# Two token tiles side by side in the MLP's first product, in a two-layer recurrent-memory transformer

## The chip, the cores and the metric

The kernel runs on one core of a Trainium2 chip. A core has a matrix engine (TensorE, here PE, with its weight loads shown apart as PEld), a vector engine (DVE), an activation engine (ACT), a general engine (POOL), and SP, which issues the DMAs. The metric is the device time of one execution in microseconds, as a median over runs.

## The reference

Four stages, one after the other, on x of 2048 tokens x 448: attention A, MLP B, attention A, MLP B, with the same weights in both layers. Each adds its result to x after a layer norm of its input.

```python
x = x + _A_ref(_layernorm(x), mem0, Wq, Wk, Wv, Wo, 32)
x = x + _B_ref(_layernorm(x), W_gate, W_up, W_down)
x = x + _A_ref(_layernorm(x), mem0, Wq, Wk, Wv, Wo, 32)
x = x + _B_ref(_layernorm(x), W_gate, W_up, W_down)

# _A_ref: 64 segments of 32 tokens, 16 heads of 256, 8 memory rows
mem = mem0
for s in range(64):
    h = concat([mem, xs])                    # 8 + 32 rows
    o = masked_attention(h, Wq, Wk, Wv) @ Wo
    mem = o[:, :8]                           # handed to the next segment
    outs.append(o[:, 8:])

# _B_ref: D = 448, F = 1792
gate, up = x @ W_gate, x @ W_up
return (relu(gate) * up) @ W_down
```

The memory rows make the 64 segments of a layer a chain: the memory of one segment must be there before the next can be computed.

## The kernel before

**Weights.** In the first 100 us the kernel multiplies Wq with Wk (tile A) and Wv with Wo (tile Bsb), so that attention needs A and Bsb alone. The MLP's weights lie in one tile named glu: Wgu holds gate in partitions 0 to 63 and up in 64 to 127, in 7 blocks of 64 input rows, and Wd holds the second product's weights.

**Work.** x is cut into 16 tiles of 128 tokens (four segments each). `chain(step)` does one step of the memory chain for both layers at once, the second layer 7 segments behind the first: a product with A (L931), evictions to Usb, turned to uT by DVE (L1102, L1109) and by copies on POOL or ACT, scores (L1125), softmax, values (L1182, L1185), the product with Bsb (L970), the result as a sum of two bf16 parts Ohi and Olo (L976 to L979), columns of it (L451 or L455), and the new memory mT. `att_group` does a quarter of the heads for the 128 token rows of a tile: product with A (L1271) to Ug, scores (L1297), softmax, values (L1182, L1185) evicted to YT, and the product with Bsb (L451, or L455 in its form of four 32-column pieces). `norm` makes the layer norm of a tile: statistics on DVE (L1202, L1203), Ln and Exp on ACT, the scaled xn on DVE (L1209), a copy of its tail on POOL (L1211), four transposing matmuls on PE, and evictions to G2 (for the MLP) or HT and HX (for attention).

**MLP.** `glu_units` computes the first product for one tile in four groups of 4, 4, 4 and 2 chunks of 128 hidden units (L1369). For each chunk 7 blocks are summed, gate in the upper and up in the lower half of PE's rows, into two PSUM banks; the moving operand has 128 columns, the tile's tokens. ACT takes relu of gate into hG (L1374), DVE multiplies it with up (L1375). `glu_down` multiplies hG with Wd (L451 or L455 again) into one bank, and `add_x` adds that to X. At each fourth chain step `tiles(step, t)` adds the work for tile t of the first layer and the MLP of tile t - 4 of the second layer, one after the other; 32 tiles pass the MLP in all. YT has two buffers that attention groups take in turn, hG has one.

**Order.** `_Sched` plans at build time. Each operation is added with what it reads and writes, and a priority from `s.now` (the step at which it is due), a level, and a shift that the string ORDER gives each part. The order of the matmul operations on PE is written out in the string LINE; the planner puts placeholder matmuls (`spin`, L1403) where it expects PE to be idle. The other engines take what is ready with the best priority when the plan is made. The program that results is fixed: each engine runs its list in order and waits on semaphores.

Of the kernel before, what the change touches and what calls it, by code (L numbers as in the profile page):

```python
# [7 lines left out]
ACT = mybir.ActivationFunctionType  # L8
# [24 lines left out]
ORDER = ("HpAPMPyEuNeA0SaAG0LeAiALVNaZuiMooJhLgmmePCRWJHARuwIrbebRcG0cyWGAAVNtfYwOc0nwyA0tUTUbj0a0rwUaVYSaqQSaXaaaJzp0aa"  # L33
         "AavSWamtqalXdaCDhsaaXMTTaNqHfkQPbpDJIyaQtvBu0uUakP0Hhaaam0aglDHFXPffJA0b0XZTLlsXz0xtZAKpWaWC0qvIMavnaBwTjApbui"
         "ZuxSVdlvZ0jSATpoOicNAevhiHGGe0aHfafWAFbdwQOhQiPTRipmXja0UpAe0glCcNdZhZTV0n0VYOlUlaBAoWZUaNXXhFzRRnaQOaflAhHuHm"
         "iwgctAngvaOhMWpDuahHgTtFp0OoKUASzDAKBlxaz0aG0ANGb0AiFoqJJuxoAYLMKAgoSIYmjtd0PdgNKT0GA0jgoCfJc0TuUT00waecBbGAqT"
         "AKwS0aYJa0OIEBpKgYJnvhnzyZ0yP0vxIAbfAfAKemIffwgaCfYUMuBlaLhaNpdAO0HKQcoorEZAgScecR0KiUFpVVTgUwVqzQ0vlOGAAjXJAd"
         "A0fkAknC00FL0cXG0O0CVUandalMqb0cwuxZjzHedgAgVAFJsXcFNBybUX0AHfGuWgWLHAyAVa0rawAE0hhMqAJbHsaXAmgHY0BAYKAsSdrkfV"
         "EJJVJI0DxucWi0AteqEmCWkzAxPrAqgcsytY0OkaHAaBFGmU0QXWOT0sVU0larr0UIVoAEdgxbOGkPXZ0W00lNIOTragAaTrDMpTTJopDZuDZA"
         "exIQtxXnfAoOqqCVyDXRHXNQwSJgTkSOyYYQ0EMqzpZkYboycvZQjjHlaZFaNAVwdEz0dMWpo0BWq0oBaLtQ00PXdseACAoaqfltC0XQLtUayA"  # L40
         "aSNOAfdHAaHbVRqNiRabKiEvt0aZAtyXrpEciNsABZfHNpX0jAJuVz0AACqjy0NBWnqSGEsBfaWTa0PIYPakbimVoxlfUD0SldXdTEXmslqpbo"
         "uiUgqkIopuFtagEaVSOvQpZS0jVRKi0rjqhuEZawSRcdxRPMmpQeFyTAdjUrgFWuzXM0rTHOqhkhHuotlvuEyWmKasUWaijtOu0lSqF0lJaaaa"
         "aa0kNZKf0aaaaaaaaaaaaaaaaaaaAAhiRNSxarWjAbjG")

SIGNS = "ABCDEFGHIJKLMNOPQRSTUVWXYZabcdefghijklmnopqrstuvwxyz0123456789+-*/=<>()[]{}.,:;!"
LINE = ("AEFOFEKJIHEFGEFELKGIEFEEEF~XENMIFHGGFAEDNDKEDGEFDDACCKKJEHGEDCCCKKIHGECDCAAAAJHHDDEABBAMIPAHFABBCBAARgfACBAEaA"
        "qBAXFAUCKSCALfBOOBAMAAYKDBZAHAGGAABUBCWBYBAAFYAADPAEDCCADIPFAAHQPDNGDEACIDCCBBDABAAWAAAKSAJAAOddHASARAXEAAA~EM"
        "A~CAggA(AeABAbAa9AZDYYACCFATAACCQPAAAMAAKKKAJJAIAHHABFBADCCAAAAAAAMSYBAKeVcKKAMR~JXAMLA~NAAAEJEADAGFZYCHCCUABB"
        "RACPASANNNAALANwMKA0DJCIHHGKGGGAGFGGAEADAABBFAAAABABAMBAYXAPJbUAJIAWAAABDDEACDCccFCAIDACAATAABQAPBARNNNAALAKLL"
        "43LAsCJOHIHBGGGAFHHeAEAEAACBBAEAAABCAATMBAWfWKAbKJSYALdAcKKAMAAEEADS7A76oGeF2CCAzBEAwAzvvvCCcGrAAsrEEAAAmkBBSi"  # L50
        "nAggJfffBIddUDdc0BaBZBBDBVAZUCLBAQQQJAABMOANNgBeAVJKaAPAIPBHZGhBXBEJADDEFWFANCAsrB~K~JxqBDAnDClLAEiiiAAgC;CggF"
        "AAADCaAAeYWAVVAAXTTBSAzBQCRQAANUNAAAKACIBHMHHAGGAFGFPAbbEAARLABUmBJYIBBJBTIIFFBOIEBA[)qGpFC/[CAB+Ej8AKED4445AA"
        "2FAE10zhgxAA1CuAtkBBqqqAgDFXAkQAahiihBBOekBBBbBJZtZZZCLXZAZYAKBAHKSAAAPUNANbMSMMMAANLKAI88EXWD-4AAT1FA4zDIDwww"
        "AdGtAttBQqQpBuPDAlCCjAADgAiffABBdcAAaaCAAAAsVAaAASmSssARRRCAAANAAAZKeAAiBBATGdTkHGQgFAEQAUAABXgNB1LBBMBFFBADA("
        "(GRFCHC-NABB7*ACe4CA222AAAZzyAzynnw2CAccrrIqGGooopHHCmFAUiaEggA-EeAKABaBZ2HHXXXDXAVCWrWWAA2bUAEAAOPAONUBBLwLLO"
        "EKAJIJ44IUUEDAyA3EAOu~KuUEDrrrAAqEoAoonEDMAAEhAmAfDCdAcAbDaEDAAXWAWWAAATpwSYARsRBCPPRPAAAALAYACAjbIAoIHRkAQaQT"
        "GAAAACSBBgLBBBIaRBEB}{IACSCC<CAB*N>A+jAA777DA6A4A44AbAi06AAAxXvvlBtttAbAEADRmmEmmDUDqjDDDgfEeFDcccAeDaAcbGkFBB"
        "XVAAaETASRXEDPPPQAANE==NAKACA8=OOVH4NBb1BAzzzAPyACvNCvuCRrAqBDAnDClpAEJiiijAAgDC5eeeAADAaAAYAArWAAATTBSApBBAmA"
        "NAAiAAZlBAHJhBAIHAADANACWLLaBkNBJgBVKKBBBFFBNAGA((FpRFC*CCF9AB*7AnDC33H42AA0A00hZxxA2fAXtCCriqqAp)ETnAAnnECQPS"
        "AohCABcdAbCaAAYYDXYAXWFVWVHBAFRACVAO5ANEMMMEXWOMEKARI66IfDd2AA0F4zBAxxxyDAAuAuuBLrAJwpAAHBlMpkBBAhhhAABeABAccD"  # L60
        "AZCCAAVAAASxSmSSARqDBAAeANMAAgAYJksjqDJVgmIVs(UAAVGGUlTAAOENAMPDbDOAABBBIyFBEBDG+9rHGDAC3ClCABy3BAwYvCuu~GDtWB"
        "rAsrAFE.voAQAlkCjBONgggQBBeAcAccSCZAYePAJBITLBRrRRRBDPIDQQAgCNAALUJAAIAMGGaAAEEEAGLABBBAwvMBBSAqDAuAnGClLBjjjK"
        "AAgCAhgC.BcAcDhAAZYCXbAAVVVAATAUTrqTAAuQCPBBNAMMMNAAKAfAIWiDAATGASEEEhYfOEQAbUDPODKDDDMAGCFC{]ItHE>AD]=HBA-AL9"
        "99AA7A88CfBG4AA07DAAyBX3wvmuAttcGsAqatspGBEEnEVrEiEipE6ggFjfffAFDgcIcTccaDH]ZDDgdXW*FVAUUHTCLSCQAaaPR+PXAfAbVD"
        "MCSARRTRAAPCARQBFBKALAAJHBHBFBADDDUADCABPHUHBbSZCFBAVEHEGGJAAABCEPCEDAMBBDBDCBAAAAABAADAAABABAAAAA")
# [420 lines left out]
NYT = 2  # L486
NHG = 1
# [24 lines left out]
class _Kernel:  # L512
# [5 lines left out]
    def __init__(self, nc, x, mem0, Wq, Wk, Wv, Wo, Wg, Wu, Wd, out):  # L518
        self.nc = nc
        self.x_d = x.rearrange("b (t p) d -> p (b t) d", p=128)  # L520
        self.out_d = out.rearrange("b (t p) d -> p (b t) d", p=128)
        self.mem0_d = mem0
        self.Wq_d = Wq.rearrange("d h e -> d (h e)")
        self.Wk_d = Wk.rearrange("d h e -> d (h e)")
        self.Wv_d = Wv.rearrange("d h e -> d (h e)")
        self.Wo_d = Wo.rearrange("h (t p) d -> p (h t) d", p=128)
        self.Wg_d, self.Wu_d, self.Wd_d = Wg, Wu, Wd
        self.s = _Sched({"C": ("C0", "C1"), "G": ("G0", "G1", "G2", "G3", "G4", "G5")})
        self.gi = 0
        self.si = 0  # L530
        self.yi = 0
        self.xi = 0

# [12 lines left out]
    def sb(self, name, shape, dtype=BF):  # L546
        return self.st.enter_context(self.nc.sbuf_tensor(name, shape, dtype))
# [4 lines left out]
    def alloc(self):  # L552
# [44 lines left out]
        self.G2 = [sb(f"G2_{i}", [128, 7, 128]) for i in range(2)]  # L597
# [30 lines left out]
        self.YT = [sb(f"YT{i}", [128, 14, 128]) for i in range(NYT)]  # L628
        self.hG = [sb(f"hG{i}", [128, NFC, 128]) for i in range(NHG)]
# [7 lines left out]
    def constants(self):  # L637
# [12 lines left out]
        hG = self.hG[0].rearrange("p a b -> p (a b)")  # L650
        hk = [("hG", 0, q) for q in range(2)]
# [60 lines left out]
    def weights(self):  # L712
# [82 lines left out]
        self.Wos += [quad(b.rearrange("p a b -> p (a b)")) for b in (*self.YT, self.hG[0])]  # L795
        self.Wos += [quad(b.rearrange("p a g b -> p (a g b)")[:, 0:4 * D]) for b in self.Ug]
        homes = [[], []] + [[("YT", y, v, h) for v in range(2) for h in range(2)] for y in range(2)] + [[("hG", 0, q) for q in range(4)]]
# [3 lines left out]
        for n, p in enumerate(self.order):  # L801
# [9 lines left out]
            for k in homes[n]:  # L811
                s.alias[k] = keys
# [432 lines left out]
    def att_group(self, l, t, g, bo):  # L1245
# [5 lines left out]
        yi = self.yi % NYT  # L1251
        si = self.yi % 2
        self.yi += 1
        Ug, YT = self.Ug[ui], self.YT[yi]
# [65 lines left out]

        for p in range(2):
# [11 lines left out]
            s.add("pe", mm_cost(*[128] * 3, 64, 64), yy, r=["PTx"] + hk, w=yb, alloc=yb, room=[("YT", yi, p, h) for h in range(2)], mode=2)  # L1333
            for h in range(2):
                t0 = 64 * p + 32 * h
                s.add(EV, ev_cost(D), copy_any(YT[:, :, t0:t0 + 32], lambda h=h, yb=yb: yb[h].ap()[:, 0:D].rearrange("p (a q) -> p a q", q=32)),
                      r=[yb[h]], w=[("YT", yi, p, h)])

        s.part()
        yk = [("YT", yi, p, v) for p in range(2) for v in range(2)]  # L1340
# [13 lines left out]
    def glu_units(self, t, g, qs, i):  # L1354
        s = self.s
        G, hG = self.G2[g], self.hG[i]
        for q in qs:
# [5 lines left out]
            def fn(E, e, two=two, q=q, n=n):  # L1363
                for c in range(n):
# [7 lines left out]
            s.add("pe", mm_cost(*[128] * (7 * n)), fn, r=[("G2", g, v) for v in range(3)] + [f"W{v}_{n}" for v, n in ((0, 6), (1, 6), (0, q), (1, q), (2, q))], w=two, alloc=two, room=[("hG", i, q)], mode=2)  # L1372
            dst = hG[:, 4 * q:4 * q + n, :].rearrange("p a b -> p (a b)")
            s.add("act", 170 + 0.833 * N, lambda E, e, dst=dst, z=two[0], N=N: E.activation(dst, z.ap()[:, 0:N], ACT.Relu), r=[two[0]], w=[("hG", i, q)])  # L1374
            s.add("dve", dv_cost(N), lambda E, e, z=two[1], N=N, dst=dst: E.tensor_tensor(dst, dst, z.ap()[:, 0:N], ALU.mult),  # L1375
                  r=[two[1]], w=[("hG", i, q)])

    def glu_down(self, t, i):
# [3 lines left out]
        hG = self.hG[i]  # L1382
        for q in range(4):
# [6 lines left out]
            s.add("pe", mm_cost(*[D] * n), fn, r=[("hG", i, q), f"Wd_{q}"], w=[bk], alloc=[bk] if q == 0 else (), also=(1,))  # L1390
# [54 lines left out]
    def mlp(self, u, g):  # L1445
        self.glu_units(u, g, (0, 1, 2, 3), 0)
        self.glu_down(u, 0)
        self.store(u)

    def tiles(self, step, t):  # L1450
# [77 lines left out]
```

## Time and profile before

| | |
|---|---|
| time, median of 3 runs | 1507.24 us (1504.69 to 1507.53) |
| the profiled execution's own time | 1510.53 us |
| its span | 1508.7 us |
| PE, DVE, ACT, POOL busy | 99%, 75%, 61%, 11% of the span |
| matmuls | 39,444, each with its weight load |
| L1369, the MLP's first product: PE busy | 190.6 us in psG and 12.4 us in psC |
| granted clock of PE | 0.999 on average |
| DMA | 34.4 MB, most of it in the first 100 us |

The page gives busy time by engine, the chain of work that ended last, and the costliest groups by line; the waits view adds up an engine's idle time by what ended it; the timeline gives starts. A matmul's end is modelled, so a line of 196 matmuls that take 216 ns each is read by starts. "Issue" is idle time in which the engine waited for nothing that the profile shows.

### The profile page before, as it was taken

What the parts mean: (1) busy time and instruction counts of PE and PEld (TensorE: products, weight loads), DVE (VectorE), ACT (ScalarE), POOL (GpSimd) and SP (SyncE); (2) the same over time, 40 slices, a digit from 0 to 9 for tenths busy, and PEclk for the clock granted to TensorE, in tenths of its full rate; (3) what the DMA queues carried; (4) which work ended last, traced back from release to release, by engine and by line L of the source; (5) the groups of instructions that cost most, each with busy time, mean ns of one, the idle gap of its engine ahead of it and who ended that gap; (6) DMA issues with size and microseconds to landing.
All of it is one profiled execution on the core that took longest, in us unless ns stands there. A gap on an engine that the chain in (4) does not pass through costs nothing.

```text
span 1508.7 us, 88102 instructions
## 1 busy us (share of the span) xinstructions
PE 1488.7 (99%) x39444; PEld 1070.2 (71%) x39444; DVE 1136.8 (75%) x3529; ACT 925.1 (61%) x2563; POOL 166.5 (11%) x652
## 2 busy tenths in 40 slices
PE   8999999999999999999999999999999999999999
PEld 6657666676767777777768677777768676777776
DVE  5657777787878887687877878678777778787764
ACT  8876566665656666566655666466655555555643
POOL 1010111111111111011110111011100111010000
PEclk9999999999999999999999999999999999999999
DMA  7612100000000000000000000000000000000000
GB/s 215 197 29 75 41 8 12 12 9 8 8 4 12 12 8 14 4 18 6 17 6 12 12 12 12 5 18 5 18 5 8 14 9 15 5 12 5 12 6 14
DMA packets 62600, 34.42 MB, mean 23 GB/s; under 512 B 31872, under 2 KB 62096, under 8 KB 62224
## 3 DMA queue, kind: packets, MB, share of 16 engines
q1 hardware_dynamic: 62224, 28.80, 7.4%
q8 instruction: 310, 5.08, 1.4%
q14 instruction: 66, 0.54, 0.1%
HBM read 21.36 MB, written 1.84 MB: 15 GB/s over the span
## 4 chain that ended last, share of the span: by engine, by line
PE 96%; ACT 2%; DVE 2%; issue 1%; POOL 0%; DVEq 0%
PE psG L1271 17%; PE psG L451 17%; PE psG L1369 12%; PE psC L970 11%; PE psC L931 9%; PE psG L455 6%; PE psG L931 4%; PE psG L758 3%; PE psG L1182 3%; PE psG L1297 3%; PE psC L451 2%; PE psC L1125 2%; PE psC L1182 1%; PE psG L745 1%; PE psG L970 1%; PE psG L1185 1%
## 5 line engine op out<-in xcount | busy, mean ns | idle before, releaser
L1271 PE MATMUL psG<-HT,A 64*128 64x128 bf16 x5016 | 288.6, 216 | 1.2 <-issue 0.8
L1271 PE MATMUL psG<-HX,A 64*128 64x128 bf16 x3762 | 269.3, 216 | 0.9 <-issue 0.7
L1271 PEld LDWEIGHTS psG<-HT,A 64*128 64x128 bf16 x5016 | 236.3, 94 | 15.4 <-issue 5.9
L441 ACT ACTIVATE Ug<-psG 64x128 bf16<-64x128 f32 (+2 forms) x430 | 155.7, 380 | 70.2 <-PE psG L1271 60.0
L1271 PEld LDWEIGHTS psG<-HX,A 64*128 64x128 bf16 x3762 | 195.8, 94 | 1.5 <-issue 1.4
L1369 PE MATMUL psG<-G,glu 64*128 64x128 bf16 x6062 | 190.6, 216 | 1.0 <-issue 0.7
L1369 PEld LDWEIGHTS psG<-G,glu 64*128 64x128 bf16 x6062 | 176.2, 94 | 11.1 <-issue 4.8
L451 PE MATMUL psG<-Bsb,YT 128*128 128x448 bf16 x850 | 182.3, 352 | 0.0
L970 PE MATMUL psC<-Bsb,YTm 128*32 128x448 bf16 x3472 | 178.4, 353 | 0.7 <-DVE YTm L444 0.3
L931 PE MATMUL psG<-A,mT 64*32 64x448 bf16 x4060 | 161.9, 350 | 2.3 <-issue 1.8
L931 PE MATMUL psC<-A,mT 64*32 64x448 bf16 x3780 | 154.5, 350 | 0.8 <-ACT mT L441 0.4
L1109 DVE STREAM_TRANSPOSE uT<-Usb 128x384 bf16<-128x384 bf16 x280 | 154.0, 551 | 0.8
L970 PEld LDWEIGHTS psC<-Bsb,YTm 128*32 128x32 bf16 x3472 | 87.6, 97 | 64.9 <-ACT YTm L441 1.4
L444 DVE CAST Ug<-psG 64x128 bf16<-64x128 f32 (+2 forms) x284 | 114.1, 414 | 15.2 <-PE psG L1271 8.0
L441 ACT ACTIVATE YT<-psG 128x448 bf16<-128x448 f32 x227 | 115.7, 543 | 10.3 <-PE psG L1185 9.0
L931 PEld LDWEIGHTS psC<-A,mT 64*32 64x32 bf16 x3780 | 78.6, 92 | 57.3 <-ACT mT L441 5.3
L451 PEld LDWEIGHTS psG<-Bsb,YT 128*128 128x128 bf16 x850 | 74.3, 97 | 56.4 <-issue 1.3
L1374 ACT ACTIVATE hG<-psG 128x512 bf16<-128x512 f32 (+1 forms) x127 | 69.0, 543 | 63.3 <-PE psG L1369 58.3
L931 PEld LDWEIGHTS psG<-A,mT 64*32 64x32 bf16 x4060 | 84.1, 92 | 22.9 <-issue 4.3
L444 DVE CAST YT<-psG 128x448 bf16<-128x448 f32 x135 | 81.5, 613 | 20.0 <-PE psG L1185 18.0
L1375 DVE TENSOR_TENSOR hG<-hG,psG 128x512 bf16<-128x512 bf16 (+1 forms) x119 | 73.1, 618 | 29.8 <-ACT hG L1374 28.7
L977 DVE TENSOR_TENSOR Olo<-psC,Ohi 128x448 bf16<-128x448 f32 x64 | 39.8, 622 | 59.1 <-ACT Ohi L976 58.9
(256 smaller groups left out, 3040.5 us busy)
## 6 DMA issues: line engine op xcount, KB each, us to landing
HR<-xn SPq DMA_DIRECT2D x128, 32.0 KB
Tsb<-Rsb SPq DMA_DIRECT2D x256, 1.5 KB
Tsb<-Rsb SPq DMA_DIRECT2D x256, 2.0 KB
Bsb<-in_A_Wq_dram SPq DMA_DIRECT2D x6, 384.0 KB
Bsb<-in_A_Wk_dram SPq DMA_DIRECT2D x6, 384.0 KB
HR<-Rsb SPq DMA_DIRECT2D x126, 1.5 KB
HR<-Rsb SPq DMA_DIRECT2D x126, 2.0 KB
X<-in_A_x_dram SPq DMA_DIRECT2D x16, 112.0 KB
```

Of the source, the lines that this page charges most:

```text
L441: return E.activation(out, i, ACT.Copy, scale=1.0 if scale is None else scale)
L444: return E.tensor_copy(out, i)
L451: return E.matmul(out, lhsT=lhsT, rhs=rhs, **k)
L455: i = E.matmul(out[q], lhsT=w, rhs=rhs, tile_position=(0, 32 * j), **k)
L931: i = E.matmul(ub[v].ap()[32 * j:32 * j + 32, 0:D], lhsT=self.mT[rw, WHERE[b], first:first + 32], rhs=cols, start=(b == 0), stop=(b == 6), ...
L970: x = E.matmul(bo.ap()[32 * j:32 * j + 32, 0:D], lhsT=self.YTm[:, q, :], rhs=self.Bsb[:, chunks[q], :], start=(i == 0), stop=(i == 13), ti ...
L1109: self.s.add("dve", 578, lambda E, e, out=out, hh=hh: E.transpose(out, heads[hh]), r=[("Usb", 2 * half + v) for v in range(2)], w=[f"uT{ha ...
L1182: return E.matmul(ps[:, n * q:n * q + n], lhsT=HR[rows, 128 * q:128 * q + 128], rhs=PT, start=True, stop=True, tile_position=(b, 0))
L1271: i = E.matmul(ub[v].ap()[:, 128 * n:128 * n + 128], lhsT=self.A[rw, b, a0:a0 + 128], rhs=HT[rw, WHOLE[b], :, 0:SEG] if CROSS[b] is None e ...
L1369: i_ = E.matmul(two[v].ap()[:, 128 * c:128 * c + 128], lhsT=self.Wgu[rw, b, f0:f0 + 128], rhs=G[rw, WHOLE[b] if CROSS[b] is None else 4 + ...
L1374: s.add("act", 170 + 0.833 * N, lambda E, e, dst=dst, z=two[0], N=N: E.activation(dst, z.ap()[:, 0:N], ACT.Relu), r=[two[0]], w=[("hG", i, ...
L1375: s.add("dve", dv_cost(N), lambda E, e, z=two[1], N=N, dst=dst: E.tensor_tensor(dst, dst, z.ap()[:, 0:N], ALU.mult), r=[two[1]], w=[("hG", ...
```

## The change

For tiles 4 to 15, the first product of the MLP is computed for tile t of the first layer and tile t - 4 of the second together. The two G2 tiles become the halves of one tile GG, and the moving operand takes both: 256 columns for each weight load. The work is cut into 7 groups of 2 chunks, each into two banks of 2 x 2 x 128 columns, and one eviction on ACT and one on DVE write both tiles' rows (L1384 in the changed kernel is the matmul). The first four tiles of the first layer and the last four of the second keep the old form (L1413). `YT` and `hG` become one tile P3 of three buffers of the same size, which attention groups (one each) and MLPs (one, or two for a pair) take in turn by `take`; who takes a buffer waits for all readers of its last holder. In `tiles` the pair's MLP, both second products and the store come ahead of the first attention group of the second layer. ORDER and LINE are new strings, so the order of PE's whole work is another.

```diff
-        self.G2 = [sb(f"G2_{i}", [128, 7, 128]) for i in range(2)]
+        self.GG = sb("GG", [128, 2, 7, 128])
+        self.G2 = [self.GG[:, i] for i in range(2)]
...
-        self.YT = [sb(f"YT{i}", [128, 14, 128]) for i in range(NYT)]
-        self.hG = [sb(f"hG{i}", [128, NFC, 128]) for i in range(NHG)]
+        self.P3 = sb("P3", [128, NSH, 14, 128])
+        self.turns = list(range(NSH))
+        self.epoch = [0] * NSH
+        self.held = [[("P3", i, 0)] for i in range(NSH)]
...
+    def take(self, parts):
+
+        i = self.turns.pop(0)
+        self.turns.append(i)
+        old = self.held[i]
+        self.epoch[i] += 1
+        self.held[i] = [("P3", i, self.epoch[i], q) for q in range(parts)]
+        return i, old, self.held[i]
...
-    def glu_units(self, t, g, qs, i):
+    def glu_units(self, tg):
+
         s = self.s
...
+        if len(tg) == 2:
+            (i, old, ka), (j, old2, kb) = sorted((self.take(7), self.take(7)), key=lambda x: x[0])
+            old = old + old2
+            for k in range(7):
+                s.part()
+                two = [self.bank("G", "C") for _ in range(2)]
+
+                def fn(E, e, two=two, k=k):
+                    for c in range(2):
+                        f0 = 128 * (2 * k + c)
+                        for b in range(7):
+                            for v in range(2):
+                                rw = slice(64 * v, 64 * v + 64)
+                                i_ = E.matmul(two[v].ap()[:, 256 * c:256 * c + 256], lhsT=self.Wgu[rw, b, f0:f0 + 128],
+                                              rhs=self.GG[rw, :, WHOLE[b] if CROSS[b] is None else 4 + CROSS[b], :],
+                                              start=(b == 0), stop=(b == 6), tile_position=(64 * v, 0))
+                    return i_
...
+                dst = self.P3[:, i:j + 1:j - i, 2 * k:2 * k + 2, :].rearrange("p t c q -> p c t q")
+                z = lambda v, two=two: two[v].ap().rearrange("p (c t q) -> p c t q", c=2, t=2)
+                w = [ka[k], kb[k]]
+                s.add("act", ev_cost(512)["act"], lambda E, e, dst=dst, z=z: E.activation(dst, z(0), ACT.Relu), r=[two[0]], w=w, room=old)
+                s.add("dve", dv_cost(512), lambda E, e, z=z, dst=dst: E.tensor_tensor(dst, dst, z(1), ALU.mult), r=[two[1]], w=w)
...
-        for u, g in groups[:1]:
-            if g == 0:
+        def first():
+            s.now = step + 3
+            for u, g in groups[:1]:
                 self.bu = self.bank("G", "C")
-            s.level = 0 if u == NT - 1 else 1
-            self.att_group(1, u, g, self.bu)
-        s.level = 1
-        if t < NT:
-            self.glu_units(t, g1, (0, 1, 2, 3), 0)
-            self.glu_down(t, 0)
-        s.now = step + 4
-        if t >= 4:
+                s.level = 0 if u == NT - 1 else 1
+                self.att_group(1, u, g, self.bu)
+            s.level = 1
+        if 4 <= t < NT:
+            s.now = step + 4
+            for x in self.glu_units([(t, g1), (t - 4, g4)]):
+                self.glu_down(*x)
+            self.store(t - 4)
+            first()
+            s.now = step + 4
+        elif t < NT:
+            first()
+            for x in self.glu_units([(t, g1)]):
+                self.glu_down(*x)
+            s.now = step + 4
+        else:
+            first()
+            s.now = step + 4
             self.mlp(t - 4, g4)
```

More of the change, by code (lines that the diff above doesn't have):

```diff
@@ L32 @@
 STEPS = "ABCDEFGHIJKLMNOPQRSTUVWXYZabcdefghijklmnopqrstuvwxyz0"
[L33 to L43, printed above, removed]
@@ L485 @@
 NUG = 2
-NYT = 2
-NHG = 1
+NSH = 3
 KZ, KT, KW = 384, 448, 576
@@ L648, in dve @@
             s.add("dve", 250, lambda E, e: fn(E), **k)
-        hG = self.hG[0].rearrange("p a b -> p (a b)")
-        hk = [("hG", 0, q) for q in range(2)]
+        hG = self.P3[:, 2].rearrange("p a b -> p (a b)")
+        hk = [("P3", 2, 0)]
         s.add("dve", 400, lambda E, e: E.memset(hG[:, 0:576], 0.0), w=hk)
@@ L794, in weights @@
         quad = lambda b: b.rearrange("p (a b) -> p a b", b=D)
-        self.Wos += [quad(b.rearrange("p a b -> p (a b)")) for b in (*self.YT, self.hG[0])]
+        self.Wos += [quad(b.rearrange("p a b -> p (a b)")) for b in (self.P3[:, i] for i in range(NSH))]
         self.Wos += [quad(b.rearrange("p a g b -> p (a g b)")[:, 0:4 * D]) for b in self.Ug]
-        homes = [[], []] + [[("YT", y, v, h) for v in range(2) for h in range(2)] for y in range(2)] + [[("hG", 0, q) for q in range(4)]]
+        homes = [[], []] + [[("P3", i, 0)] for i in range(NSH)]
         homes += [[("Ug", u, k, v) for k in range(3) for v in range(2)] + [("Ug", u, 3, v, hh) for v in range(2) for hh in range(2)] for u in range(2)]
@@ L811, in weights @@
             for k in homes[n]:
-                s.alias[k] = keys
+                if k[0] == "P3":
+                    self.held[k[1]] = [k] + keys
+                else:
+                    s.alias[k] = keys
         self.A_all = [("A", p, hh, k) for p in range(NPAIR) for hh in range(2) for k in range(7)]
@@ L1319, in att_group @@
         s.add(EV, ev_cost(256, fast=True), copy_any(PT[0:104, :], lambda: bp.ap().bitcast(BF)[0:104, 0:256]), r=[bp], w=["PTx"])
+        yi, old, yk = self.take(4)
+        YT = self.P3[:, yi]
         for p in range(2):
@@ L1332, in att_group @@
             hk = [q for h in range(2) for q in self.hr_keys(l, 4 * t + 2 * p + h)]
-            s.add("pe", mm_cost(*[128] * 3, 64, 64), yy, r=["PTx"] + hk, w=yb, alloc=yb, room=[("YT", yi, p, h) for h in range(2)], mode=2)
+            s.add("pe", mm_cost(*[128] * 3, 64, 64), yy, r=["PTx"] + hk, w=yb, alloc=yb, room=old, mode=2)
             for h in range(2):
@@ L1336, in att_group @@
                 s.add(EV, ev_cost(D), copy_any(YT[:, :, t0:t0 + 32], lambda h=h, yb=yb: yb[h].ap()[:, 0:D].rearrange("p (a q) -> p a q", q=32)),
-                      r=[yb[h]], w=[("YT", yi, p, h)])
+                      r=[yb[h]], w=[yk[2 * p + h]], room=old)
         s.part()
-        yk = [("YT", yi, p, v) for p in range(2) for v in range(2)]
         bk = [q for q in self.B_all if q[1] in pairs]
@@ L1352, in add_x @@
         self.s.add("dve", dv_cost(D), lambda E, e: E.tensor_tensor(X[:, :], bk.ap()[:, 0:D], X[:, :], ALU.add), r=[bk], w=[("X", t % NX)])
-    def glu_units(self, t, g, qs, i):
+    def glu_units(self, tg):
         s = self.s
-        G, hG = self.G2[g], self.hG[i]
-        for q in qs:
+        if len(tg) == 2:
[14 more added lines that the diff above has]
+                    return i_
+                q = k // 2
+                s.add("pe", mm_cost(*[256] * 14), fn, r=[("G2", g, v) for g in range(2) for v in range(3)] + [f"W{v}_{n}" for v, n in ((0, 6), (1, 6), (0, q), (1, q), (2, q))],
+                      w=two, alloc=two, room=old, mode=2)
+                dst = self.P3[:, i:j + 1:j - i, 2 * k:2 * k + 2, :].rearrange("p t c q -> p c t q")
[3 more added lines that the diff above has]
+                s.add("dve", dv_cost(512), lambda E, e, z=z, dst=dst: E.tensor_tensor(dst, dst, z(1), ALU.mult), r=[two[1]], w=w)
+            at = {0: (i, ka), 1: (j, kb)}
+            return [(t, *at[g]) for t, g in tg]
+        (t, g), = tg
+        G = self.G2[g]
+        i, old, keys = self.take(4)
+        for q in range(4):
             n = 4 if q < 3 else 2
@@ L1371, in fn, with glu_down @@
                 return i_
-            s.add("pe", mm_cost(*[128] * (7 * n)), fn, r=[("G2", g, v) for v in range(3)] + [f"W{v}_{n}" for v, n in ((0, 6), (1, 6), (0, q), (1, q), (2, q))], w=two, alloc=two, room=[("hG", i, q)], mode=2)
-            dst = hG[:, 4 * q:4 * q + n, :].rearrange("p a b -> p (a b)")
-            s.add("act", 170 + 0.833 * N, lambda E, e, dst=dst, z=two[0], N=N: E.activation(dst, z.ap()[:, 0:N], ACT.Relu), r=[two[0]], w=[("hG", i, q)])
+            s.add("pe", mm_cost(*[128] * (7 * n)), fn, r=[("G2", g, v) for v in range(3)] + [f"W{v}_{n}" for v, n in ((0, 6), (1, 6), (0, q), (1, q), (2, q))], w=two, alloc=two, room=old, mode=2)
+            dst = self.P3[:, i, 4 * q:4 * q + n, :].rearrange("p a b -> p (a b)")
+            s.add("act", 170 + 0.833 * N, lambda E, e, dst=dst, z=two[0], N=N: E.activation(dst, z.ap()[:, 0:N], ACT.Relu), r=[two[0]], w=[keys[q]], room=old)
             s.add("dve", dv_cost(N), lambda E, e, z=two[1], N=N, dst=dst: E.tensor_tensor(dst, dst, z.ap()[:, 0:N], ALU.mult),
-                  r=[two[1]], w=[("hG", i, q)])
-    def glu_down(self, t, i):
+                  r=[two[1]], w=[keys[q]])
+        return [(t, i, keys)]
+    def glu_down(self, t, i, keys):
         s = self.s
@@ L1381, in glu_down @@
         bk = self.bank("G", "C")
-        hG = self.hG[i]
+        hG = self.P3[:, i]
         for q in range(4):
@@ L1445, in mlp @@
     def mlp(self, u, g):
-        self.glu_units(u, g, (0, 1, 2, 3), 0)
-        self.glu_down(u, 0)
+        for x in self.glu_units([(u, g)]):
+            self.glu_down(*x)
         self.store(u)
```

59 lines of the change are left out of this document (36 added, 23 removed).

## The prediction

> **What bounds the kernel now.** I read the page first, then the idle time of PE by what ended it, then the costliest groups, then the timeline where one operation follows another.
>
> ```profile
> PE 1488.7 (99%) x39444; PEld 1070.2 (71%) x39444; DVE 1136.8 (75%) x3529; ACT 925.1 (61%) x2563; POOL 166.5 (11%) x652
> PE 96%; ACT 2%; DVE 2%; issue 1%; POOL 0%; DVEq 0%
> ```
>
> PE is busy 99% of the span, and the chain that ended last runs through it for 96%. Both lines flatter PE a little, since a matmul's modelled end covers short pauses. So I count starts instead. The timeline gives the paces:
>
> ```profile
> 1495.79 1.68 PE L451 MATMUL psG<-glu,hG 128*128 128x448 bf16 x8
> 1497.40 5.65 PE L1369 MATMUL psG<-G,glu 64*128 64x128 bf16 x196
> ...
> 68.05 0.28 PE L1036 MATMUL psC<-Bsb,YTm 128*32 128x256 bf16 x2
> 68.05 0.27 PE L1036 MATMUL psC<-glu,YTm 128*32 128x256 bf16 x2
> 68.16 0.28 PE L1036 MATMUL psC<-Bsb,YTm 128*32 128x256 bf16 x2
> ```
>
> The next operation after the 196 matmuls of L1369 starts at 1502.98. That is 5.58 us for 98 pairs (the two row halves of the array work side by side) and one change of tile shape. The eight L451 matmuls tell the two apart: they take 1.61 us to the next start, eight paces of 189 ns and 93 ns for the change of shape. So a pair of 128 columns costs 56 ns. L1036 is the only line that streams 256 columns; its groups of four start 109 ns apart (68.05 to 68.16, and the same over its run). The paces lie on one line in the column count (56, 109, 189 for 128, 256, 448).
>
> Adding these paces over all 39,444 matmuls in their order, side-by-side ones counted once, 25 ns for the short ones and 93 ns at each of the 574 changes of shape, gives 1464.0 us. From first to last matmul start the trace has 1504.2. The missing 40.2 us are PE idle: 10.6 in the first 100 us (cold clock and weight loading), 8.6 at instructions that wait on a semaphore between 100 and 350 us, 2.4 at such instructions after 350 us, and 18.6 inside runs that wait for nothing after 100 us. The waits view shows the same kinds:
>
> ```profile
> PE psG L931 <- issue: 1.8, 4, 0.7
> PE psG L1297 <- POOL HT L1003: 0.7, 2, 0.4
> PE psC L455 <- DVE Olo L979: 0.7, 2, 0.5
> PE psG L451 <- POOL xn L1211: 0.5, 1, 0.5
> ```
>
> Each is small. A change can therefore win only by taking paces off PE, or out of these 40 us, and it loses wherever PE gets too little work between giving a result away and needing it back.
>
> **Merged product.** For the 12 tile pairs, 24 tiles of 196 matmuls with 128 columns (4,704) become 2,352 with 256 columns; the other 8 tiles keep 1,568. In slots: 2,352 of 56 ns go, 1,176 of 109 ns come, 1,176 x (112 - 109) = 3.5 us less. The bounds: L1369's slots average 56.5 ns over the run, some at 66, which gives 4.7; a slot at exactly the line through the rows gives 2.8. The moving operand now has two pieces of 128 columns; L1271 reads four pieces of 32 and L931's weights are strided as well, both at the same pace, so I charge nothing. If the weight loads (94 ns each, halved in number here) set the 56 ns, the gain would be far larger; that is a rival.
>
> **Changes of shape.** In the built order of the changed kernel the array changes shape 596 times, 22 more: 22 x 93 ns = 2.0 us more.
>
> **Rest of PE's work.** The same matmuls stand in it, apart from the placeholder matmuls that the planner puts where it expects PE idle: 22 of 448 columns for 18 and 45 of 128 for 40, 4 x 189 + 5 x 56 ns = 1.0 us more. What changes between 128-wide and four 32-wide forms (L451, L455) costs the same, 189 ns and 4 side by side in 179 to 189.
>
> **Runs that wait for nothing.** 14.3 of the 18.6 us are 50 single pauses of 0.12 to 1 us, mostly in L931 and L1271, called issue. They go with the number of instructions fetched, I assume; 6% fewer matmuls make 0.7 us less (between 0, and 1.2 for L1369's own share).
>
> **ACT and DVE.** A pair needs 7 evictions of 512 on each where it had 8 (six of 512, two of 256): ACT 7 x 596 against 6 x 596 + 2 x 382 ns, DVE 7 x 682 against 6 x 682 + 2 x 410. About 0.15 us less per pair on each, at nothing, since both stand idle 39% and 25% of the span. The strided destination is 128-element runs; Ug is written in runs of 32 at the same 686 ns.
>
> **The ring.** A pair holds two of three buffers until both second products (L451, L455) have read them, and attention groups share the third. That limits the order, and adds no semaphore wait on PE: reader and next writer's matmul are both on PE, reader first. Its price is in the hand-offs. SP has the same 1,029 DMAs, and the moved store is 112 KB on a queue that is nearly empty after 100 us (5% DMA share): nothing. POOL has two copies more.
>
> **Hand-offs.** This term decides. For each waiting matmul I took the longest chain of ACT, DVE, POOL instructions back to the matmul that starts it, with the rows' mean durations and some 50 ns for each passing of a semaphore, and set it against the paces that stand between them on PE. Before: too little work at 22 places in the first 100 us (4.5 us short in sum), at 31 places from 100 to 350 us (7.4 us), at 2 places after that (0.02 us). The trace's idle at waiting matmuls for the same stretches is 6.8, 8.6 and 2.4, so the tally tells where it happens, at about 1.15 of its size. The changed kernel's order gives 14 places (3.7 us), 23 places (5.8) and 22 places (5.5). The new ones are, for example:
> - about 450 us of PE work: after the last output matmul of the memory chain PE has some 0.7 us of other work before the transposing matmuls (L455 before) need Olo, while Ohi (ACT, 543 ns), Olo (DVE, 622), its tail copy (179) and three hand-overs take 1.5: 0.8 us. Two placeholders stand there, and right behind it the next product of the chain needs POOL's two mT copies, 0.7 us short.
> - about 811 us: the transposes of the normalised tile (L451) need POOL's copy of xn (309 ns), which stands on POOL behind two uT copies of the memory chain (289 each); these need Usb's eviction (607) and the tl transpose (290). PE has 0.5 us of work there: 1.4 us short, and everything on PE stands behind these four transposes.
> Scaled by 1.15 the three stretches give -0.9, -1.9 and +6.3, 3.5 us together. The tally leaves out that an engine may still be at an earlier instruction. With each engine's own order added, the places after 350 us come to 21 us in sum, but places that follow each other share one delay; the largest of each cluster make about 5, and the memory chain's own cluster near 290 us was worth twice its largest in the trace. I take +5.0 for the term, nearer the plain tally that the trace bears out; its ends are 0 and +15.
>
> **Sum.** -3.5 + 2.0 + 1.0 - 0.7 + 5.0 = +3.8 us. The profiled execution took 1510.53 us (span 1508.7 and 1.8 around it), 3.3 above the median of the runs, 1507.24; I set the difference on the median: 1511.0 us. No change is what lies within 0.2%, 3.0 us: 1504.2 to 1510.3.
>
> **Rivals.**
> *Hand-offs are covered (faster).* The places after 350 us hang on POOL and DVE being late; in the trace before, POOL is 11% busy and PE lost only 2.4 us there. If those places cost at most 1 us and the first 350 us keep the 2.8 us that their tally promises, the sum is -3.5 + 2.0 + 1.0 - 0.7 - 1.8 = -3.0: 1504.2, and with the merged slots at their upper bound 1503. It decides where the new places cost under 1 us together. Against it: the placeholders at 450 us, and shortages that come from dependencies alone. Chance 0.15.
> *They cost about half (no change).* Term near +1 to +3, 1507 to 1510. For it: 1464.0 us of PE work before against 1463.5 after. Chance 0.25.
> *They pile up (much slower).* DVE is 75% busy on average and 80% around 400 us; when PE halts at the places near 450, 790 and 811 us, evictions queue behind the norm. At the full 21 us: 1526. The two clusters near 290 us in the trace argue against, which cost a third of their full sum. Chance 0.08.
> *Weight loads set the pace (much faster).* L1369's loads are busy 176.2 us beside 190.6 of its matmuls. If the loads made the 56 ns, a merged slot could cost as little as one old slot: 1,176 x 56 = 66 us off, 1507.2 - 65.9 + 7.3 = 1449. Against it: 109 ns at 256 columns in L1036 and a straight line through 448. Chance 0.02.
> The Trainium skill, "TensorE: Matmul & The Clock Gate", section "Back-to-back issue gap", says that weight load and matmul together set the spacing, about 81 ns at 128 columns and 131 at 512. By an estimate on the line between them a merged slot would take 98 ns in place of 162, 75 us less in all, near 1432; the trace's 56 ns at 128 columns does not agree.
> That the merge would not happen at all is excluded, since the built order has it.
>
> **How the numbers follow.** The likeliest case, hand-offs at +4 or more without piling up, has 0.50. Faster: 0.15 + 0.02 = 0.17. Same: 0.25. Slower: 0.50 + 0.08 = 0.58. The range goes from 1503, the faster rival's lower end, to 1520, the forecast's with the hand-offs near their upper end (+14); it leaves out the load rival, most of the piling up, and a little on either side.
>
> **What would show it.** In the profile after: the merged product's matmuls in pairs 109 ns apart, so about 10.7 us for a whole pair of tiles; PE's waits after 350 us grown to about 7 us, with Olo, POOL's xn and mT among their releasers; issue a little lower; ACT and DVE 2 us less busy each. I am wrong if the waits after 350 us stay near 2 us (then faster), if the pairs stand much closer than 109 ns, or if another engine's queue holds PE for over 1 us at many tiles.

## The result, and the profile after

The changed kernel takes 1513.22 us (median of 7 runs, 1509.26 to 1514.73) against 1505.58 for the kernel before (7 runs, 1503.69 to 1507.53; the three runs with the median of 1507.24 are among them): ratio 1.0048, 95% interval 1.0039 to 1.0058. It is slower, by 7.6 us in the medians where +3.8 was forecast. The profiled execution took 1511.89 us.

The first lines of the page and its chain hardly differ from those of before. PE is still "99%" busy; only the chain has lost two points on PE and given one to DVE:

```profile
PE 1488.9 (99%) x37095; PEld 1052.1 (70%) x37095; DVE 1135.2 (75%) x3515; ACT 922.8 (61%) x2551; POOL 166.7 (11%) x654
PE 94%; DVE 3%; ACT 2%; issue 1%; POOL 0%; DVEq 0%
```

That is a warning for this kind of kernel: 2,349 matmuls fewer, and the busy time says nothing, since ends are modelled and short idle times vanish under them. The waits view, cut to the time after 350 us, shows it (us in total, times, longest):

```profile
PE psG L451 <- DVE xn L1223: 2.7, 1, 2.7
PE psG L451 <- POOL xn L1225: 1.2, 2, 0.8
PE psG L455 <- POOL xn L1225: 0.8, 2, 0.6
PE psG L1310 <- POOL HT L1017: 0.4, 1, 0.4
```

Before, the same stretch had 0.5 us for POOL's xn and 0.2 for Px, and nothing else above 0.2 but issue. In the changed kernel PE waits for the layer norm's xn at five places, for 4.7 us. (The view counts from a matmul's modelled end, so it shows less than the count by starts in the table below.) One of them takes 2.7 us, near 845 us:

```profile
841.67 0.22 PE L1199 MATMUL psG<-PTx,HR 40*128 40x64 bf16 x4
844.55 0.40 PE L451 MATMUL psG<-ident,xn 128*128 128x128 bf16 x4 [2.65 <-DVE xn L1223]
```

And the merged product runs as it should. The timeline has 196 matmuls of 256 columns for a whole pair of tiles, and the next operation 10.81 us later: less one change of shape, 98 slots of 109 ns.

```profile
976.16 10.87 PE L1384 MATMUL psG<-GG,glu 64*128 64x256 bf16 x196
986.97 0.93 PE L451 MATMUL psG<-glu,P 128*128 128x448 bf16 x4
```

The same count as in the prediction (paces in PE's order, against the starts in the trace), for two profiled executions of each kernel, in us; the second figures are from the first experiment:

| | before | changed |
|---|---|---|
| sum of the paces | 1464.0 | 1464.3 |
| waits on a semaphore, first 100 us | 6.8, 6.7 | 6.9, 7.4 |
| the same, 100 to 350 us | 8.6, 8.6 | 7.5, 7.5 |
| the same, after 350 us | 2.4, 2.4 | 9.8, 10.3 |
| pauses without a semaphore, all | 22.4, 19.2 | 17.1, 15.8 |
| the execution's own time | 1510.5, 1507.3 | 1511.9, 1511.6 |

In each stretch the waits repeat to within 0.5 us from one execution to the next. The pauses without a semaphore do not, and the times of one kernel differ by as much. So the waits are compared from the profiles, and the total from the medians.

### The profile page after: what moved, and what is told of

It reads as the page before. It is cut to its first block, busy times and chain, and to the rows that moved or that the text cites. A ratio compares the mean times of both kernels' runs of the same rounds, so it can differ in the third digit from the quotient of the medians.

```text
span 1510.1 us, 83371 instructions
## 1 busy us (share of the span) xinstructions
PE 1488.9 (99%) x37095; PEld 1052.1 (70%) x37095; DVE 1135.2 (75%) x3515; ACT 922.8 (61%) x2551; POOL 166.7 (11%) x654
## 4 chain that ended last, share of the span: by engine, by line
PE 94%; DVE 3%; ACT 2%; issue 1%; POOL 0%; DVEq 0%
PE psG L451 17%; PE psG L1284 16%; PE psC L984 11%; PE psG L1384 9%; PE psC L945 8%; PE psG L455 6%; PE psG L945 4%; PE psG L1196 3%; PE psG L769 3%; PE psG L1413 3%; PE psG L1310 2%; PE psC L451 2%; PE psC L1139 2%; PE psC L1196 1%; PE psG L756 1%; PE psC L1284 1%
## 5 line engine op out<-in xcount | busy, mean ns | idle before, releaser
L451 PE MATMUL psG<-Bsb,P 128*128 128x448 bf16 x931 | 199.1, 354 | 0.0
L945 PE MATMUL psG<-A,mT 64*32 64x448 bf16 x4060 | 151.6, 350 | 0.2
L945 PE MATMUL psC<-A,mT 64*32 64x448 bf16 x3780 | 145.3, 350 | 0.9 <-ACT mT L441 0.3
L1384 PE MATMUL psG<-GG,glu 64*128 64x256 bf16 x2310 | 133.3, 269 | 0.0
L441 ACT ACTIVATE P<-psG 128x448 bf16<-128x448 f32 x250 | 125.2, 543 | 10.7 <-PE psG L1199 9.7
L451 PEld LDWEIGHTS psG<-Bsb,P 128*128 128x128 bf16 x931 | 82.8, 98 | 65.0 <-issue 2.5
L1384 PEld LDWEIGHTS psG<-GG,glu 64*128 64x128 bf16 x2310 | 110.5, 94 | 16.2 <-issue 1.5
L945 PEld LDWEIGHTS psG<-A,mT 64*32 64x32 bf16 x4060 | 79.2, 92 | 22.4 <-ACT mT L441 1.4
L1017 POOL COPY HT<-mT 128x32 bf16<-128x32 bf16 x126 | 23.2, 211 | 600.1 <-DVE mT L1007 600.1
L1394 ACT ACTIVATE P<-psG 128x512 bf16<-128x512 f32 x83 | 49.6, 597 | 61.6 <-PE psG L1384 61.3
L1395 DVE TENSOR_TENSOR P<-P,psG 128x512 bf16<-128x512 bf16 x82 | 56.0, 683 | 39.9 <-ACT P L1394 39.3
```

Source lines behind the costliest of these rows:

```text
L441: return E.activation(out, i, ACT.Copy, scale=1.0 if scale is None else scale)
L451: return E.matmul(out, lhsT=lhsT, rhs=rhs, **k)
L945: i = E.matmul(ub[v].ap()[32 * j:32 * j + 32, 0:D], lhsT=self.mT[rw, WHERE[b], first:first + 32], rhs=cols, start=(b == 0), stop=(b == 6), ...
L1384: i_ = E.matmul(two[v].ap()[:, 256 * c:256 * c + 256], lhsT=self.Wgu[rw, b, f0:f0 + 128], rhs=self.GG[rw, :, WHOLE[b] if CROSS[b] is None ...
L1394: s.add("act", ev_cost(512)["act"], lambda E, e, dst=dst, z=z: E.activation(dst, z(0), ACT.Relu), r=[two[0]], w=w, room=old)
L1395: s.add("dve", dv_cost(512), lambda E, e, z=z, dst=dst: E.tensor_tensor(dst, dst, z(1), ALU.mult), r=[two[1]], w=w)
```

## The experiments

The theory is that of the prediction: PE's own work is unchanged in sum, and the loss is places in PE's new order where PE gets too little work between giving a result away and needing what ACT, DVE and POOL make of it. The rivals: the merge or the ring themselves cost something; or the pauses called issue make the difference.

**Both kernels once more.** No edit.

> The kernel before, unchanged, for a second profile. Hand-off theory: PE's waits on semaphores stand where they stood (about 8.6 us from 100 to 350 us, 2.4 us after), since the order is fixed; the time is that of before, ratio 1.000. Rival (the difference comes from pauses without a semaphore, called issue): these differ from one profiled execution to the next by several us (18.6 us after 100 us in the first profile), and the waits too.

> The changed kernel, unchanged, for a second profile. Hand-off theory: about 9.8 us of PE waits after 350 us again, 2.7 us of it at one place near 845 us; time 1.005 of before. Rival (issue): the 12.6 us of pauses without a semaphore after 100 us move by several us, and the time with them, while the waits are no steadier.

Before against itself: 0.9999 (0.9990 to 1.0007). The changed kernel: 1513.39 us against 1507.26, 1.0043 (1.0029 to 1.0057). The second profiles are the second figures in the table above. The longest wait of the changed kernel came back word for word:

```profile
PE psG L451 <- DVE xn L1223: 2.7, 1, 2.7
```

The pauses without a semaphore moved by 3.2 us in the kernel before, and its profiled execution's time by the same 3.2 us. In the changed kernel they are lower, not higher, so they don't make it slower.

**The merge taken apart.** Each matmul of 256 columns as two of 128, in the same place of the same order.

```diff
-                        for b in range(7):
+                        for u, b in ((u, b) for u in range(2) for b in range(7)):
                             for v in range(2):
                                 rw = slice(64 * v, 64 * v + 64)
-                                i_ = E.matmul(two[v].ap()[:, 256 * c:256 * c + 256], lhsT=self.Wgu[rw, b, f0:f0 + 128],
-                                              rhs=self.GG[rw, :, WHOLE[b] if CROSS[b] is None else 4 + CROSS[b], :],
+                                o = 256 * c + 128 * u
+                                i_ = E.matmul(two[v].ap()[:, o:o + 128], lhsT=self.Wgu[rw, b, f0:f0 + 128],
+                                              rhs=self.GG[rw, u, WHOLE[b] if CROSS[b] is None else 4 + CROSS[b], :],
```

> The changed kernel with each merged matmul of 256 columns given as two of 128, in the same place of the same order, each with its own weight load; nothing else. Prediction's pace (56 ns for 128 columns, 109 for 256): 1,176 slots of 109 become 2,352 of 56, 3.5 us slower than the changed kernel, so about 1.0072 of before. Rival (the merge itself is what costs, by its strided operand or its long slots): no slower or faster than the changed kernel, 1.005 or less. Rival (weight loads set the pace at 128 columns): 60 us or more slower, 1.045.

1517.29 us, 1.0069 of before (1.0056 to 1.0082): 3.9 us above the changed kernel on the same chip, where 3.5 was expected. The intervals of the two ratios touch, so the trace has to carry the size. The rival of no slowdown (1.005 or less) lies below the interval. The same pair of tiles as above, in this kernel's timeline:

```profile
979.11 11.12 PE L1385 MATMUL psG<-GG,glu 64*128 64x128 bf16 x392
990.16 0.93 PE L451 MATMUL psG<-glu,P 128*128 128x448 bf16 x4
```

It takes 11.05 us from start to start in place of 10.81: 196 slots of 56 ns, 0.24 us more per pair of tiles and 2.9 us for all twelve. The merge is a gain, of about 3 us, in this order. The waits view of the split kernel after 350 us also has two lines that neither profile of the changed kernel shows:

```profile
PE psG L1385 <- issue: 0.9, 3, 0.5
PE psC L1139 <- ACT mC L441: 0.5, 1, 0.5
```

So part of the 3.9 us may not be pace. Weight loads don't set the pace: with twice as many of them this stretch grew by 2%, where the rival needed 60 us in all.

**One operation moved.** The four transposing matmuls near 845 us go behind the next four operations of PE's order (2.4 us of work). The other engines are planned anew from there, with small differences.

```diff
-        out += left
+        out += left; i = next(n for n, o in enumerate(out) if o.idx == 5092); out.insert(i + 4, out.pop(i))
```

> The changed kernel with one operation of PE's order, the four transposing matmuls that wait 2.7 us near 845 us, moved behind the next four operations (2.4 us of PE work). Hand-off theory: that wait falls below 0.5 us; part of it comes back two operations later, where the memory chain's scores need uT (up to 1.4 us, as those scores stood only 0.2 us short before); net 1 to 2.5 us faster than the changed kernel, 1.0035 to 1.0045 of before. Rival (the waits are noise of the profile, the time comes from elsewhere): no change against the changed kernel, 1.005.

1511.36 us, 1.0026 (1.0017 to 1.0036), 2.0 us below the changed kernel on the same chip and so inside the 1 to 2.5 us expected. The ratio is lower than expected, as the changed kernel's own was 1.0043 there. The two intervals overlap, so here too the trace has to carry the size. The 2.7 us wait is gone from the view; the other places stand where they stood:

```profile
PE psG L451 <- POOL xn L1225: 1.2, 2, 0.8
PE psG L455 <- POOL xn L1225: 0.8, 2, 0.6
```

A piece of it came back as expected: the planner put three placeholder matmuls there (L1449, 0.6 us), and PE halts 0.3 us at the memory chain's scores, two operations on. The 2.7 us less these two make 1.8:

```profile
846.15 0.40 PE L451 MATMUL psG<-ident,xn 128*128 128x128 bf16 x4
846.38 0.54 PE L1449 MATMUL psC<-A 128*128 128x448 bf16 x2
847.23 0.57 PE L1139 MATMUL psC<-HT,uT 128*128 128x40 bf16 x16 [0.31 <-ACT HT L441]
```

**The same fault in the kernel before.** Three transposes of a normalised tile moved forward in its order; no merge, no ring.

```diff
-        out += left
+        out += left; [out.insert(i - k, out.pop(i)) for x, k in ((2775, 4), (3970, 6), (6186, 4)) for i in [next(n for n, o in enumerate(out) if o.idx == x)]]
```

> The kernel before (no merge, no ring) with three operations of PE's order moved forward: the transposes of a normalised tile at three places (about 450, 665 and 965 us), each 2.9 us of PE work earlier, so that each is some 2.9 us short of xn. The planner fills part of each gap with placeholder matmuls (34 of 448 columns, 6.4 us). Hand-off theory: places alone, without merge or ring, make 7 to 9 us: 1.0045 to 1.006 of before. Rival (the loss of the change belongs to the ring or the merged slots, and PE makes up for such waits later): under 3 us, below 1.002.

1512.57 us against 1506.72, 1.0036 (1.0022 to 1.0050): 5.4 us from three moved operations. It is less than the 7 to 9 expected, and above the rival's 3, as the interval begins at 3.3. The view shows what is left as waits; the rest are 34 placeholders and six more changes of shape, 7.0 us by the paces.

```profile
PE psG L455 <- POOL xn L1211: 1.9, 3, 0.9
```

By the trace the three places cost 8.9 us, and the time rose by 5.4. In this profile the pauses without a semaphore are 16.4 us, lower than in both profiles of the kernel before; that is where the difference could lie, though one execution doesn't show it.

**Another order, all else kept.** Another pair of strings ORDER and LINE, found by moving single operations and shifts while the plan's end time fell; nothing else differs.

```diff
-ORDER = ("NjAPMPasAIF0GPiRBwQhAzSKCPACXUfdMFiOdikLzKNTZLPwIsAJuUrMocDmteGVEVcdZnkDTYAEadJ0yMShnxn0dtsaZQLaQvoaVFQa0tk0aa"
...
-LINE = ("AEENFNEEFGFFFFEEHJIJF~cEEEFFEMLHGEFGFEFELMJFFHFFEFEMALGGFDEDDEDKAAIGFFDDBBCBKIDGDBBBBKABAHJGAEAAAAAFNffBABAEAZ"
...
+ORDER = ("NjAPbRklkrYkIottAUkdIoSKKPC0DnlyVbgEfqmpVSETZLbZCaAQNeryecwuXeCVEVc0dkqgfOEcqlAbQNShnxn0ftPZpInkbknanBWVXgq0Vo"
...
+LINE = ("AFEFNEGEHFGEEFEEHJIGFEEF~ZEEENMLIGIFFFEELLGFEEEEEEEMMKJFGFEEEEAKKDFGFEEDEACLJABCEDDCBKCBLAHBEBDCAAAFNffAABNAEA"
...
```

> The changed kernel with another ORDER and LINE alone, found by moving operations of PE's order and shifts of priorities; merge, ring and all else stay. Array shape changes 577 times in place of 596 (1.8 us less), and 16 places after 350 us are 2.9 us short by their dependencies, where the changed kernel has 22 with 5.5; the 2.7 us place is gone. Hand-off theory: 4 to 6 us faster than the changed kernel, 1.0003 to 1.0015 of before, waits after 350 us at 4 to 6 us. Rival (merge or ring cost something that no order removes): still above 1.003.

1506.61 us (11 runs), 0.9994 of before (0.9984 to 1.0003). The loss of the change is gone with the order alone, so neither the merge nor the ring is what it comes from. By the count of paces and starts this kernel has 1462.2 us of work, 2.1 less than the changed kernel (577 changes of shape for 596), waits of 7.5 us after 350 us where the changed kernel has 9.8 and 10.3, and 12.7 us of pauses after 100 us, where the changed kernel had 12.6. Both parts of the expectation were missed: the waits stayed above 4 to 6 us, and the time fell by more than 4 to 6 us, by 7 to 8 in the ratios. The count places 4 to 5 of these, 2.1 in the work and 2.1 to 3.1 in all waits together (22.1 us where the changed kernel has 24.2 and 25.2). The other 2 to 4 us have no place in it, and this kernel is as fast as the one before although PE waits 5 us longer after 350 us. So the order as the cause is shown, and the waits as the whole of it are not. The 2.7 us place is gone; what remains are again places where PE waits for POOL's xn:

```profile
PE psG L452 <- POOL xn L1226: 1.2, 2, 0.8
PE psG L456 <- POOL xn L1226: 0.8, 2, 0.6
```

**The same with three of the plan's costs set right.** The planner took 203 ns for xn's first 64 columns on DVE, where the trace has 291, 236 for POOL's copy of them, where it has 309, and similarly less for the copies of uT. With the measured durations a new pair of strings was sought. The kernel with the first new order ran beside it. A new search with the old costs was not run, so what the costs did and what a second search would have done by itself can't be told apart.

```diff
-            self.s.add(("pool", "act"), ev_cost(128), copy_any(to, of), r=[("tl", half)], w=[("uT2", half, hh)], at=hh, cross=True, **P)
+            self.s.add(("pool", "act"), {"pool": 298, "act": 308}, copy_any(to, of), r=[("tl", half)], w=[("uT2", half, hh)], at=hh, cross=True, **P)
...
-            s.add("dve", dv_cost(of.stop - of.start, fast=True) + 20,
+            s.add("dve", dv_cost(of.stop - of.start, fast=True) + (20 if of.start else 108),
...
-        s.add("pool", 236, lambda E, e: E.tensor_copy(xn[:, KT + 64:KW], xn[:, KT:KT + 64]), r=[("xn", i, 0)], w=[("xnt", i)])
+        s.add("pool", 309, lambda E, e: E.tensor_copy(xn[:, KT + 64:KW], xn[:, KT:KT + 64]), r=[("xn", i, 0)], w=[("xnt", i)])
...
-ORDER = ("NjAPMPasAIF0GPiRBwQhAzSKCPACXUfdMFiOdikLzKNTZLPwIsAJuUrMocDmteGVEVcdZnkDTYAEadJ0yMShnxn0dtsaZQLaQvoaVFQa0tk0aa"
+ORDER = ("NjAPbvtEpICLLJw0HXilZ0SGKQlhEnLaHBgEgqmBXSETZLYRAaBaSenvMcKu0bCVEVc0FiPYWWTemlAUADShnxn0frOSmeIPDlFafYVOPru00a"
...
-LINE = ("AEENFNEEFGFFFFEEHJIJF~cEEEFFEMLHGEFGFEFELMJFFHFFEFEMALGGFDEDDEDKAAIGFFDDBBCBKIDGDBBBBKABAHJGAEAAAAAFNffBABAEAZ"
+LINE = ("AHGENEGFIFIFFEENEIIHHGEE~ZEEEMMJIGGGFEFELLGFEEEEEEEMMLKGEFFFEELLAFIEEFDDADCAKIDDEBBBBBJBLAHGCACABAGAggNAABNAEA"
```

> The changed kernel with three of its planner's costs set to the durations in the trace (xn's first 64 columns on DVE 291 ns where the plan had 203, POOL's copy of them 309 for 236, the copies of uT on POOL and ACT 298 and 308), and ORDER and LINE searched anew under these costs. The theory: what is left of the loss, 7.5 us of waits after 350 us in the kernel with the first new order, comes from these prices being too low, so that the plan puts POOL's xn later than PE needs it and does not know it. The planner's own end time with the true costs falls by 4.6 us from that order to this one, so the waits after 350 us fall to 3 to 4 us and the time to about 1502 us, 0.997 of before. PE's own work stays at 1462.2 us (581 changes of shape). Rival one: the plain tally of the prediction (given away, needed again, PE's work in between) gives 3.7 us after 350 us where it gave 2.9 for the first new order, and 7.5 for 6.4 in the stretch from 100 to 350 us; if it is the better guide, the waits stay at 7 to 8 us and the time at 1507 to 1509. Rival two: the waits fall as the theory says but the pauses without a semaphore rise by the same, and the time stays at 1506 to 1507.

> The kernel with the first new order once more, on the same chip as the next one, so that the two can be compared: 0.9994 of before again, within 0.001, and the same waits after 350 us (7.5 us) to some tenths.

1505.56 us (12 runs), 0.9982 of before (0.9970 to 0.9993), and 1508.25 us, 0.9998 (0.9989 to 1.0008), for the first new order beside it, whose waits view has the same two lines as above. With the corrected costs and the order found under them the changed kernel has the lowest ratio of all that were run, 0.18% below the kernel before. Its interval does not reach 1, but the 0.18% is less than the 0.2% up to which a change counts here as none. Some 1502 us had been expected. Neither rival fits: the waits are below the first one's 7 to 8 us, the time below the second one's 1506 to 1507. The theory was half right. One place is repaired, POOL's xn at 476 us (0.6 to 0.2); here are the new kernel's lines:

```profile
PE psG L452 <- POOL xn L1226: 1.2, 2, 0.8
PE psG L456 <- POOL xn L1226: 0.4, 2, 0.2
```

The place of 0.8 us stayed. So the waits after 350 us fell from 7.5 to 6.5 us, not to 3 or 4, and all waits together from 22.1 to 20.6. That is 1.5 of the 2.7 us between the two medians, whose intervals just overlap; the rest isn't settled. Near 1328 us the timeline shows why the place stayed. ACT has the scale at 1326.73, DVE does another tile's statistics and a softmax step first, and POOL's copy then takes 0.61 us, where the median of its 64 is 0.316:

```profile
1326.53 0.62 DVE L1217 BATCH_NORM_STATS2 lnst<-X 128x6 f32<-128x448 bf16 x1
1327.06 0.30 DVE L1322 TENSOR_REDUCE stx<-Tx 128x4 f32<-128x160 f32 x1
1327.28 0.29 DVE L1224 TENSOR_SCALAR xn<-X,lnst 128x64 bf16<-128x64 bf16 x1
...
1327.63 0.61 POOL L1226 COPY xn<-xn 128x64 bf16<-128x64 bf16 x1 [2.88 <-DVE xn L1224]
```

No fixed cost in the plan has that. The slow copy is no accident of one execution: in all ten profiles, those of the kernel before among them, one copy of xn between 1322 and 1339 us takes 0.61 or 0.62 us. In the kernel before it did not hold PE, which came to the transposes of xn only at 1327.58:

```profile
1325.65 0.62 POOL L1211 COPY xn<-xn 128x64 bf16<-128x64 bf16 x1 [3.83 <-DVE xn L1209]
```

Why it takes twice its median was not tested. The order of the kernel before was not sought anew with these costs, so nothing here says that it could not gain as well.

## Why the prediction was right

Forecast slower, at 1511.0 us in a range of 1503 to 1520; measured 1513.22. The difference against the kernel before came out at twice the forecast (7.6 for 3.8 in the medians; the interval of the ratio makes it 5.9 to 8.7). The direction and the reason were right: a new order with too little work on PE at some hand-offs costs more than the merge saves. The size was not, and that slower was forecast at all hung on a choice: with the plain tally's own 3.5 us for the hand-offs in place of the 5.0 taken, the sum is +2.3, which the prediction counts as no change. Step by step:

- **Merged product, -3.5 us.** Right: 109 ns a slot in the trace, 2.9 us by the timeline of the split kernel and 3.9 by its time. (The lower bound of 2.8 comes to 3.3 by the rounded paces beside it.) The rival of the weight loads falls with it. So does the estimate made beside it from the Trainium skill's "TensorE: Matmul & The Clock Gate", section "Back-to-back issue gap" (81 ns at 128 columns): the split kernel would have been about 75 us slower by that, and was 3.9.
- **Changes of shape, +2.0, and placeholders, +1.0.** The counts were in the built order; the price of a change of shape is 93 ns in the changed kernel's trace too. PE's own work is 1464.3 us where it was 1464.0; these two terms and the merged product had put it at 1463.5, and the 0.8 us between are not placed.
- **Runs that wait for nothing, -0.7.** Undecided. Two profiles of each kernel give 20.8 us before and 16.5 after in the mean, but they move by 3 us between executions of one kernel, and the total time doesn't show a gain of that size. An estimate shows why: the two profiled executions lay 5.0 and 0.0 us above their medians before, and 1.3 and 1.8 below them after. If that is all in the pauses, at the medians they are 17.4 and 19.2 before and 18.4 and 17.6 after, which leaves no gain. With it the account nearly closes: 0.3 us more work and 7.0 more waits, against 7.6 and 6.1 us in the medians. The reason given, fewer instructions to fetch, was not tested.
- **ACT, DVE, ring and queues at nothing.** DVE and ACT are 1.6 and 2.3 us less busy, about 2 as predicted. No waiting time of PE in the profile is put down to a reader of P3. The ring alone was not tried; the reordered kernel keeps it and loses nothing.
- **Hand-offs, +5.0.** This is the term that was too small. The three stretches were forecast at -0.9, -1.9 and +6.3 by the plain tally; measured are +0.4, -1.1 and +7.7, together +7.0. The scale was one reason: 1.15 is what the stretch from 100 to 350 us alone gives (8.6 for 7.4). The three stretches together had 17.8 us for 11.9 short, which is 1.49, and by that the term would have been 4.6; after 350 us the trace of the changed kernel has 10 us where the tally had 5.5. The places named were right, what held PE there only in part. At 475 us in the trace (450 of PE's work) Olo and POOL's mT were named with 0.8 and 0.7 us. By the starts they took 0.1 and 0.2; xn just ahead took 0.8, and POOL's HT between them over 0.4:

```profile
474.94 0.41 PE L455 MATMUL psG<-ident,xn 128*32 128x128 bf16 x16 [0.60 <-POOL xn L1225]
476.96 0.57 PE L1310 MATMUL psG<-HT,Ug 128*128 128x40 bf16 x16 [0.39 <-POOL HT L1017]
```

  At 845 us the plain tally had 1.4 us, by POOL's queue alone. POOL's copy was done at 843.78. DVE was the one that came late, with the second half of xn, as the timeline shows (DVE's instructions, and POOL's copy): the memory chain's eviction and transposes, at 0.3 to 0.6 us each, stand ahead of both halves (843.14 and 844.12).

```profile
841.45 0.58 DVE L444 CAST Usb<-psC 128x448 bf16<-128x448 f32 x1
841.96 0.56 DVE L1123 STREAM_TRANSPOSE uT<-Usb 128x384 bf16<-128x384 bf16 x1
842.45 0.27 DVE L1116 STREAM_TRANSPOSE tl<-Usb 128x128 bf16<-128x128 bf16 x1
842.64 0.53 DVE L1123 STREAM_TRANSPOSE uT<-Usb 128x384 bf16<-128x384 bf16 x1
843.10 0.12 DVE L1166 RECIPROCAL str<-str 128x2 f32<-128x2 f32 x1
843.14 0.31 DVE L1223 TENSOR_SCALAR xn<-X,lnst 128x64 bf16<-128x64 bf16 x1
843.36 0.57 DVE L1123 STREAM_TRANSPOSE uT<-Usb 128x384 bf16<-128x384 bf16 x1
843.54 0.24 POOL L1225 COPY xn<-xn 128x64 bf16<-128x64 bf16 x1
843.86 0.35 DVE L1169 TENSOR_SCALAR Pr<-Tr,str 128x40 bf16<-128x40 f32 x2
844.12 0.37 DVE L1223 TENSOR_SCALAR xn<-X,lnst 128x384 bf16<-128x384 bf16 x1
```

  The prediction had said that the tally leaves out an engine that is still at an earlier instruction, and with each engine's own order it had 21 us in sum. The measured 7.7 after 350 us lies between the 6.3 and the 21, nearer the plain tally. The first 350 us were trusted too much: the plain tally promised 2.8 us there, and 0.7 came.
- **Rivals.** That the new hand-offs would be covered (0.15) or cost half (0.25) both fall with the waits after 350 us, 10 us where 2.4 had been. They did not pile up to the 21 us either.

## What to carry to other kernels

On an engine that is fed without a gap, an operation is worth its pace, start to start, and what counts besides is how much of its own work lies between each result it gives away and the place where it needs the answer. Merging two streams that share weights saved no more than 3 us of 1507 here, because the moving columns and not the weight loads set the pace; the new order that it came with lost more than twice that, by the trace at hand-offs of 0.2 to 2.7 us each. So when a change brings a new order, judge the two apart: before calling the idea slower, repair the order, and compare the plan's costs with the durations in the trace. Here the same merge was 0.4 to 0.5% slower in one order, level in a second and 0.18% faster in a third.

## What was not expected of the hardware

The waits on semaphores nearly repeat from one profiled execution to the next (2.4 and 2.4, 9.8 and 10.3 us in sum after 350 us, the longest 2.7 both times), while in the kernel before the pauses inside runs that wait for nothing moved by 3.2 us, and the execution's time with them. A single profiled execution can therefore be several microseconds off its kernel's median (1510.53 against 1505.58 here), and still show the long waits to the tenth.
